# DMA transposes, LN2 statistics on GpSimd and own buffers for the last chunks in a pre-LN attention and gated-MLP block

## The chip, the cores and the metric

The kernel runs on one core of a Trainium2 chip. The metric is device microseconds of one execution. Before the change the kernel took 938.5 us (median of three runs, 938.18 to 938.94).

## The reference, cut to what matters

```python
def _A_ref(x, wqkv, wo):              # 2048 rows, 640 columns, 32 heads of 20
    q, k, v = split(x @ wqkv)
    p = softmax(q k^T * 20 ** -0.5)
    return (p v) @ wo
def _B_ref(x, w_gate, w_up, w_down):  # 640 -> 1728 -> 640
    return (gelu(x @ w_gate) * (x @ w_up)) @ w_down
h  = x + _A_ref(layernorm(x), ...)
h2 = h + _B_ref(layernorm(h), ...)    # this layernorm is "LN2" below
```

(Names shortened; the cuts are of reshapes and dtypes.) All inputs are bf16. There are 2048 x 2048 x 32 exponentials, and that decides how the kernel is built.

## The kernel before

The kernel plans itself. A small list scheduler in Python takes every operation with a modelled duration, the engine it runs on, what it reads and writes, and a priority; it simulates the five engines and writes the resulting order into the program. The program gives each engine its own queue in that fixed order, with waits on semaphores. So an edit of one part can change the order of everything that comes after it.

The query rows are split into chunks of 512, 512, 256, 256, 256, 128 and 128 rows (chunks 0 to 6). Attention of chunk c on ScalarE (the exponentials) runs beside the background work of earlier chunks: output projection, residual addition, LN2 and the MLP. VectorE computes a part of the exponentials as well, with integer arithmetic, in pairs of tiles of seven instructions. Priorities are numbers, lower first:

```python
P_QK, P_PV, P_PRO, P_EPI, P_BG = 0, 1, 1.5, 2, 3

def transposes(src, rkeys, dst, wkey, banks, prio, evac, after=()):
    bk = Bank(*banks)                       # one of the two PSUM banks for background work
    for a in range(NA):                     # five 128 x 128 transposes on TensorE
        op("pe", lambda eng, a=a: eng.transpose(bank16(bk, D)[:, 128*a:128*a+128],
                                                src[:, a*128:(a+1)*128], ident[:]), ...)
    if evac == "act": ...                   # the last chunk ("tail"): ScalarE evacuates
    else:
        op("dve", lambda eng: eng.tensor_copy(dst, v()), c_dve(D, 0.54), prio, ...)

def base(c):                                # which of four row-tile buffers a chunk starts at
    return 2 * (c % 2) if CHUNKS[c][1] < 512 else 0

def post(c, banks, tail):
    p = P_EPI if tail else P_BG
    for tt in range(tb, tb + nt):           # per 128 rows
        transposes(o_nat[:, tt, :], ..., oT[...], ..., P_EPI, ev)     # attention output
        for hf in range(2):                 # output projection, then residual addition
            list(chain(bk, key, 320, [(oT[...], wo[...]) for a in range(NA)], ..., p))
            op("dve", ... h_sb = psum + h_sb ..., p)
        ln_stats(h_sb[:, tt, :], t, ..., p)                            # bn_stats, bn_aggr
    ln_rsqrt(q0 // 128, nt, p, table=tail)  # 14 tiny VectorE operations: 1/sqrt by Newton steps
    for tt in range(tb, tb + nt):
        ln_apply("dve", h_sb[:, tt, :], xn_t[:, t % 2, :], ...)
        transposes(xn_t[:, t % 2, :], ..., hnT[...], ..., p, ev)       # LN2 output
    # gate matmuls -> VectorE copies -> GELU in batches on ScalarE -> up matmuls, product on
    # VectorE -> down matmuls -> residual addition on VectorE -> store      (all at P_BG)
```

Equal priorities are served in the order of creation.

Of the kernel before, what the change touches and what calls it, by code (L numbers as in the profile page):

```python
# [317 lines left out]
def bass_sequential_preLN__mha_block__glu_gated_geglu__prompt_kernel(  # L318
# [12 lines left out]
    with ExitStack() as es:  # L331
# [186 lines left out]
        def ln_rsqrt(t0, n, prio, table=False, sqrt=False):  # L518

            y = rs[:, t0:t0 + n]  # L520
            a, b = nw[:, 0, 0:n], nw[:, 1, 0:n]
            ts = range(t0, t0 + n)
            k16, ks = ("mv16", t0), ("sd16", t0)
            rk = [("rs", t) for t in ts]
            d = lambda fn, r, w: op("dve", fn, 0.17, prio, reads=r, writes=w)
            d(I("tensor_copy", mv16[:, t0:t0 + n, :], mv[:, t0:t0 + n, :]), [("mv", t) for t in ts], [k16])
            d(I("tensor_scalar", sd16[:, t0:t0 + n], mv16[:, t0:t0 + n, 1], LN_EPS, None, ALU.add), [k16], [ks])
            d(I("tensor_copy", mu[:, t0:t0 + n], mv16[:, t0:t0 + n, 0]), [k16], [("mu", t) for t in ts])
            if sqrt:
                op("act", I("activation", sd16[:, t0:t0 + n], sd16[:, t0:t0 + n], ACT.Sqrt), 0.2, 1, reads=[ks], writes=[ks])  # L530
                d(I("reciprocal", y, sd16[:, t0:t0 + n]), [ks], rk)
                return
            if table:
                op("act", I("activation", sd16[:, t0:t0 + n], sd16[:, t0:t0 + n], ACT.Sqrt), 0.2, -1, mode="sqrt", reads=[ks],
                   writes=[ks])
                d(I("reciprocal", y, sd16[:, t0:t0 + n]), [ks], rk)
                return
            d(I("tensor_copy", a, sd16[:, t0:t0 + n]), [ks], ["nw0"])
            d(I("tensor_scalar", b.bitcast(I32), a.bitcast(I32), 1, None, ALU.logical_shift_right), ["nw0"], ["nw1"])
            d(I("tensor_scalar", y.bitcast(I32), b.bitcast(I32), -1.0, RSQRT_MAGIC, ALU.mult, ALU.add), ["nw1"], rk)  # L540
            for _ in range(2):
                d(I("tensor_tensor", b, y, y, ALU.mult), rk, ["nw1"])
                d(I("scalar_tensor_tensor", out=b, in0=b, scalar=-0.5, in1=a, op0=ALU.mult, op1=ALU.mult),
                  ["nw0", "nw1"], ["nw1"])
                d(I("scalar_tensor_tensor", out=y, in0=b, scalar=1.5, in1=y, op0=ALU.add, op1=ALU.mult),
                  ["nw1"] + rk, rk)
            d(I("tensor_tensor", sd16[:, t0:t0 + n], a, y, ALU.mult), ["nw0"] + rk, [ks])
            d(I("reciprocal", y, sd16[:, t0:t0 + n]), [ks], rk)

        def ln_apply(eng, src, dst, dkey, t, rkeys, prio):  # L550
            if eng == "act":
# [6 lines left out]
        def transposes(src, rkeys, dst, wkey, banks, prio, evac, after=()):  # L558
            bk = Bank(*banks)
            key = ("bk", id(bk), sc_id())  # L560
            for a in range(NA):
                op("pe", lambda eng, a=a: eng.transpose(  # L562
                    bank16(bk, D)[:, 128 * a:128 * a + 128], src[:, a * 128:(a + 1) * 128], ident[:]),
                   0.055, prio, mode="full", reads=list(rkeys) + ["ident"], writes=[key], acq=[bk] if a == 0 else [],
                   after=tuple(sc.rd.get(wkey, ())) if a == 0 else ())
            v = lambda: bank16(bk, D).rearrange("p (a e) -> p a e", a=NA)
            if evac == "act":
                op("act", lambda eng: eng.activation(dst, v(), ACT.Copy), c_act(D), prio, reads=[key],
                   writes=[wkey], rel=[bk], after=after)
            else:  # L570
                op("dve", lambda eng: eng.tensor_copy(dst, v()), c_dve(D, 0.54), prio, reads=[key], writes=[wkey],
                   rel=[bk], after=after)

        _id = [0]

# [191 lines left out]
        while i < len(tiles):  # L767
# [4 lines left out]
            nd = D_PER_SLOT[c] if s_ else D_SLOT0  # L772
            units.append(tiles[i:i + len(bs)])
            ubank.append(bs[0])
            i += len(bs)
            want = min(nd, (k[0] - D_FIRST) * nd // D_SPAN + 1) if k[0] >= D_FIRST else 0
            if k[1] < want and tiles[i][0] == s_:
                dtile.append(tiles[i])
# [158 lines left out]


        def base(c):
            return 2 * (c % 2) if CHUNKS[c][1] < 512 else 0  # L940

        def epilogue(s_, bk):
            s = s_ % 2
# [29 lines left out]
        def prefetch(c):  # L973
# [1 line left out]
            nt = nq // 128  # L975
            tb = base(c)
            op("sp", I("dma_start", h_sb[:, tb:tb + nt, :], x_hbm[q0:q0 + nq, :].rearrange("(t p) d -> p t d", p=128)), 0.08, P_EPI,
               writes=[("h", tb + tt, hf) for tt in range(nt) for hf in range(2)], sem="xr", lat=2.0 + nq * 0.0034,
               after=tuple(e_ops) + tuple(w_readers) if c == 0 else ())

        def post(c, banks, tail):
# [1 line left out]
            q0, nq = CHUNKS[c]  # L983
            nt = nq // 128
            tb = base(c)
            kb = 7 * (tb // 2)
            first = tuple(e_ops) + tuple(last_qk[0]) + tuple(d_ops) if c == 0 else ()
            ev = "act" if tail else "dve"
            for tt in range(tb, tb + nt):
                t = q0 // 128 + tt - tb  # L990
                i = t % 2
                transposes(o_nat[:, tt, :], [("on", g, tt) for g in range(NG)], oT[:, :, tt * 128:(tt + 1) * 128],
                           ("hnT", tt), banks, P_EPI, ev, after=first)
                for hf in range(2):
                    bk = Bank(*banks)
                    key = ("bk", sc_id())
# [13 lines left out]
            for tt in range(tb, tb + nt):  # L1010
                t = q0 // 128 + tt - tb
                ln_apply("dve", h_sb[:, tt, :], xn_t[:, t % 2, :], ("xn", t % 2), t, [("h", tt, 0), ("h", tt, 1)], p)
                transposes(xn_t[:, t % 2, :], [("xn", t % 2)], hnT[:, :, tt * 128:(tt + 1) * 128], ("hnT", tt),
                           banks, p, ev, after=first)
            p = P_BG
            hk = [("hnT", tt) for tt in range(tb, tb + nt)]
            hdone = []
# [16 lines left out]
            def cols(k):  # L1034
                return min(512, (NF - k * fn_) * nq)

            if tail:
                for k in range(nb):
                    i = k % 2
                    bg, kg = mms(k, wg, "wg", hdone[k - 2:k - 1] if k >= 2 else ())  # L1040
                    w = cols(k)
                    s16, fv = zb[:, i, 0:w], ha_f[:, 512 * (kb + k):512 * (kb + k) + w]
                    op("act", lambda eng, bg=bg, s16=s16, w=w: eng.activation(s16, bank(bg, w), ACT.Gelu_apprx_tanh),
                       c_act(w), -1, mode="gelu", reads=[kg], writes=[("zb", i)], rel=[bg])
                    bu, ku = mms(k, wu, "wu", ())
                    hdone.append(op("dve", lambda eng, bu=bu, s16=s16, fv=fv, w=w: eng.tensor_tensor(
                        fv, s16, bank(bu, w), ALU.mult), c_dve(w), p, reads=[ku, ("zb", i)], writes=[("ha", kb + k)],
                        rel=[bu]))
            else:

                cp, gl = [], []
                for k in range(nb):
                    bg, kg = mms(k, wg, "wg", tuple(sc.rd.get(("ha", kb + k), ())))
                    w = cols(k)
                    fv = ha_f[:, 512 * (kb + k):512 * (kb + k) + w]
                    cp.append(op("dve", lambda eng, bg=bg, fv=fv, w=w: eng.tensor_copy(fv, bank(bg, w)), c_dve(w), p,
                                 reads=[kg], writes=[("ha", kb + k)], rel=[bg], after=first))
                for ks in [list(range(i, min(i + 4, nb))) for i in range(0, nb, 4)]:
                    w = 512 * (ks[-1] - ks[0]) + cols(ks[-1])
                    fv = ha_f[:, 512 * (kb + ks[0]):512 * (kb + ks[0]) + w]  # L1060
                    gl.append(op("act", I("activation", fv, fv, ACT.Gelu_apprx_tanh), c_act(w) + 0.04, -1, mode="gelu",
                                 reads=[("ha", kb + k) for k in ks], writes=[("ha", kb + k) for k in ks], after=cp))
                for k in range(nb):
                    w = cols(k)
                    fv = ha_f[:, 512 * (kb + k):512 * (kb + k) + w]
                    bu, ku = mms(k, wu, "wu", (sc.lw[("ha", kb + k)],))
                    hdone.append(op("dve", lambda eng, bu=bu, fv=fv, w=w: eng.tensor_tensor(fv, fv, bank(bu, w),  # L1067
                                                                                                 ALU.mult),
                                    c_dve(w), p, reads=[ku, ("ha", kb + k)], writes=[("ha", kb + k)], rel=[bu]))
            for tt in range(tb, tb + nt):  # L1070
                t = q0 // 128 + tt - tb
                i = t % 2
                for hf in range(2):
                    bk = Bank(*banks)
                    key = ("bk", sc_id())
                    for f in range(NF):
                        o = 512 * kb + f * nq + (tt - tb) * 128
                        op("pe", lambda eng, f=f, o=o, hf=hf, bk=bk: eng.matmul(  # L1078
                            bank(bk, 320), ha_f[:, o:o + 128], wd[:, f, hf * 320:(hf + 1) * 320],
                            start=(f == 0), stop=(f == NF - 1)), c_mm(320), p, mode="full", util=0.133, reads=[("ha", kb + f // fn_), "wd", "wdz"],  # L1080
                           writes=[key], acq=[bk] if f == 0 else [], after=hdone[-2:] if f == 0 else ())
                    op("dve", lambda eng, bk=bk, tt=tt, hf=hf, i=i: eng.tensor_tensor(
                        ob[:, i, hf * 320:(hf + 1) * 320], bank(bk, 320), h_sb[:, tt, hf * 320:(hf + 1) * 320], ALU.add),
# [86 lines left out]
```

## Time and profile before

The page of the kernel before, its busy times and its chain of waits by engine:

```profile
PE 860.0 (92%) x10297; PEld 365.5 (39%) x10297; DVE 829.1 (88%) x1807; ACT 883.7 (94%) x799; POOL 12.8 (1%) x33
...
ACT 77%; PE 15%; DVE 8%; issue 1%; DVEq 0%
```

PE is TensorE's matmuls, PEld its weight loads, DVE VectorE, ACT ScalarE, POOL GpSimd. Three engines look full at once, so the share of the whole span decides nothing. It has to be split by stage. Windows of the kernel before, each with its length, the busy time of each engine, the granted clock and the DMA share:

```profile
core 0: us, PE busy (x) PEld busy (x) DVE busy (x) ACT busy (x) POOL busy (x), PEclk, DMA share, GB/s
...
475.00:690.00 215.00, 200.05 (x2663) 82.13 (x2661) 197.30 (x420) 214.94 (x189) 0.00 (x0) 1.00 0.03 8
...
797.00:850.00 53.00, 49.77 (x1151) 31.52 (x1149) 48.69 (x116) 52.94 (x46) 0.00 (x0) 1.00 0.03 9
...
887.00:912.00 25.00, 21.49 (x231) 15.91 (x219) 16.25 (x48) 10.83 (x10) 0.00 (x0) 1.00 0.06 19
912.00:939.00 27.00, 23.87 (x341) 21.31 (x341) 10.29 (x23) 6.16 (x9) 0.00 (x0) 1.00 0.05 16
```

In the middle ScalarE is busy for all but 0.06 us of 215. After 887 us it idles and TensorE works. That last stretch is the tail, and what fills it is seen in ScalarE's timeline, where the GELU batches (written `rege<-rege`) tell how late the MLP of each chunk is:

```profile
350.76 6.46 ACT L339 ACTIVATE rege<-rege 128x2048 bf16<-128x2048 bf16 x4
...
579.24 6.46 ACT L339 ACTIVATE rege<-rege 128x2048 bf16<-128x2048 bf16 x4
...
727.74 3.28 ACT L339 ACTIVATE rege<-rege 128x2048 bf16<-128x2048 bf16 x2 [1.37 <-DVE rege L1056]
...
807.31 3.28 ACT L339 ACTIVATE rege<-rege 128x2048 bf16<-128x2048 bf16 x2
...
888.74 3.28 ACT L339 ACTIVATE rege<-rege 128x2048 bf16<-128x2048 bf16 x2
...
894.26 1.45 ACT L339 ACTIVATE rege<-ps 128x1536 bf16<-128x1536 f32 x1
```

These are chunks 0 to 4 (start in us, duration, and in brackets the idle time before it and who ended it); the last line is the last exponential, which ends at 895.7. The last chunk's residual rows are fetched late. The queue of DMA issues before:

```profile
839.65 0.34 SPq L339 DMA_DIRECT2D rege<-in_A_x_dram  x1
...
907.06 0.34 SPq L339 DMA_DIRECT2D rege<-in_A_x_dram  x1
```

The load at 907 us is that of chunk 6, which shares its buffer with chunk 4 and so waits for chunk 4's last read.

### The profile page before, as it was taken

To read this page: it belongs to the slowest core of one execution; us is meant where nothing else is said; L and a number is where in the kernel's file an instruction comes from. 1 tells how busy PE (TensorE), PEld (TensorE's weight loads), DVE (VectorE), ACT (ScalarE), POOL (GpSimd) and SP (SyncE) were. 2 spreads that over 40 slices of the span, in tenths; PEclk is the share of its full clock that TensorE was granted. 3 is DMA by queue.
4 is the path that set the end of the run, shared out by engine and by line. 5 is a ranking of instruction groups with operands and counts; after the bars stand their busy time and mean duration, and the time that the engine had idled before them with its cause. 6 is when DMAs were issued, how large, how long until landed. Compare 5 with 4: busy or idle time off the path is not lost.

```text
span 939.2 us, 23514 instructions
## 1 busy us (share of the span) xinstructions
PE 860.0 (92%) x10297; PEld 365.5 (39%) x10297; DVE 829.1 (88%) x1807; ACT 883.7 (94%) x799; POOL 12.8 (1%) x33
## 2 busy tenths in 40 slices
PE   3998999999998999998898998999999899999998
PEld 2432322222222222332243333344434446566577
DVE  7859999999899998987799999798999989989953
ACT  6899999999999999999999999999999999999931
POOL 5000000000000000000000000000000000000000
PEclk9999999999999999999999999999999999999999
DMA  7311010322630000001000000000000000000000
GB/s 253 91 24 40 19 52 18 89 65 65 198 124 1 1 2 1 1 22 37 1 2 1 2 1 1 1 3 29 30 2 1 2 20 13 3 17 10 3 22 16
DMA packets 22046, 30.12 MB, mean 32 GB/s; under 512 B 1964, under 2 KB 19464, under 8 KB 21944
## 3 DMA queue, kind: packets, MB, share of 16 engines
q1 hardware_dynamic: 21944, 28.63, 9.9%
q8 instruction: 80, 1.31, 0.6%
q14 instruction: 22, 0.18, 0.1%
HBM read 20.12 MB, written 8.09 MB: 30 GB/s over the span
## 4 chain that ended last, share of the span: by engine, by line
ACT 77%; PE 15%; DVE 8%; issue 1%; DVEq 0%
ACT pts L339 50%; ACT rege L339 26%; PE ps L1027 4%; PE ps L614 3%; PE ps L850 2%; PE ps L1078 2%; PE ps L339 2%; DVE rege L339 2%; DVE qt_all L339 2%; ACT L339 1%; DVE rege L810 1%; DVE stats L339 1%; PE ps L562 1%; DVE qt_all L810 0%; DVE kt_all L339 0%
## 5 line engine op out<-in xcount | busy, mean ns | idle before, releaser
L339 ACT ACTIVATE pts<-ps 128x1536 bf16<-128x1536 f32 x480 | 574.0, 1383 | 6.1 <-PE ps L850 4.3
L850 PE MATMUL ps<-qt_all,kt_all 32*128 32x256 bf16 (+2 forms) x3584 | 303.3, 289 | 42.7 <-ACT pts L339 28.1
L339 ACT ACTIVATE rege<-ps 128x1536 bf16<-128x1536 f32 x239 | 300.6, 1383 | 4.5 <-PE ps L339 3.1
L850 PEld LDWEIGHTS ps<-qt_all,kt_all 32*128 32x128 bf16 x3584 | 95.7, 92 | 276.4 <-ACT pts L339 163.9
L339 DVE TENSOR_TENSOR qt_all<-qt_all 128x1024 bf16<-128x1024 bf16 (+1 forms) x240 | 164.3, 685 | 3.2
L1027 PE MATMUL ps<-rege,regw 128*128 128x256 bf16 (+2 forms) x980 | 152.9, 289 | 9.5 <-ACT rege L339 4.3
L339 PE MATMUL ps<-pts,v_all 128*21 128x256 bf16 (+2 forms) x2098 | 139.2, 291 | 0.5 <-DVE rege L339 0.5
L810 DVE TENSOR_SCALAR rege<-ps 128x512 int16<-128x512 f32 x154 | 105.5, 685 | 27.5 <-PE ps L850 26.5
L339 DVE TENSOR_SCALAR qt_all<-qt_all 128x1024 bf16<-128x1024 int16 (+1 forms) x288 | 116.0, 419 | 2.0
L339 PE MATMUL ps<-rege,v_all 128*21 128x256 bf16 (+2 forms) x1294 | 113.3, 292 | 0.0
L1027 PEld LDWEIGHTS ps<-rege,regw 128*128 128x128 bf16 x980 | 72.8, 97 | 63.5 <-issue 20.8
L614 PE MATMUL ps<-regw 128*128 128x512 bf16 (+1 forms) x360 | 87.6, 354 | 2.0 <-DVE v_all L747 0.7
L1078 PE MATMUL ps<-regw,rege 128*128 128x320 bf16 x448 | 78.0, 301 | 1.9 <-DVE rege L1067 0.8
L810 DVE TENSOR_SCALAR qt_all<-ps 128x512 int16<-128x512 f32 x96 | 65.7, 687 | 4.0 <-PE ps L850 2.9
L339 DVE TENSOR_SCALAR rege<-rege 128x1024 int16<-128x1024 int16 (+2 forms) x166 | 67.3, 422 | 1.1
L339 DVE TENSOR_TENSOR rege<-rege 128x1024 bf16<-128x1024 bf16 (+3 forms) x103 | 65.7, 645 | 0.9
L339 PE MATMUL ps<-kt_all,zer 128*32 128x512 bf16 x740 | 65.7, 389 | 0.0
L339 PEld LDWEIGHTS ps<-pts,v_all 128*21 128x21 bf16 x2098 | 50.2, 91 | 37.5 <-issue 31.0
L1078 PEld LDWEIGHTS ps<-regw,rege 128*128 128x128 bf16 x448 | 36.9, 98 | 32.6 <-issue 15.2
L339 PEld LDWEIGHTS ps<-rege,v_all 128*21 128x21 bf16 x1294 | 41.1, 91 | 19.7 <-issue 13.8
L614 PEld LDWEIGHTS ps<-regw 128*128 128x128 bf16 x360 | 28.7, 99 | 45.8 <-issue 21.9
L1067 DVE TENSOR_TENSOR rege<-rege,ps 128x512 bf16<-128x512 bf16 (+1 forms) x53 | 35.9, 679 | 10.5 <-PE ps L1027 9.6
(92 smaller groups left out, 596.7 us busy)
## 6 DMA issues: line engine op xcount, KB each, us to landing
rege<-in_A_x_dram SPq DMA_DIRECT2D x6, 640.0 KB, 5.1
q_rows<-regw SPq DMA_DIRECT2D x20, 128.0 KB, 1.7
out_dram<-rege SPq DMA_DIRECT2D x16, 160.0 KB, 2.1
regw<-in_B_w_gate_dram SPq DMA_DIRECT2D x1, 2160.0 KB, 12.6
regw<-in_B_w_up_dram SPq DMA_DIRECT2D x1, 2160.0 KB, 17.6
regw<-in_B_w_down_dram SPq DMA_DIRECT2D x1, 2080.0 KB, 23.0
kt_all<-k_rows SPq DMA_DIRECT2D x12, 160.0 KB
qt_all<-q_rows SPq DMA_DIRECT2D x12, 160.0 KB
```

The lines of the kernel that those rows point to most:

```text
L339: return lambda eng: getattr(eng, method)(*args, **kwargs)
L562: op("pe", lambda eng, a=a: eng.transpose(bank16(bk, D)[:, 128 * a:128 * a + 128], src[:, a * 128:(a + 1) * 128], ident[:]), 0.055, prio, ...
L614: yield op("pe", lambda eng, l=l, r=r, k=k: eng.matmul(bank(bk, n), l, r, start=(k == 0), stop=(k == len(steps) - 1)), c_mm(n), prio, mode ...
L810: d_ops.append(op("dve", lambda eng: eng.tensor_scalar(v[:, 512 * h:512 * h + 512], bank(b), EXP_MUL, -32000.0, ALU.mult, ALU.max), c_dve( ...
L850: return lambda eng: eng.matmul(out()[:, kk * nq:(kk + 1) * nq], kt_all[32 * j:32 * j + 32, g, kt * 128:(kt + 1) * 128], qt_all[32 * j:32 ...
L1027: op("pe", lambda eng, a=a, f=f, fi=fi: eng.matmul(bank(bk)[:, fi * nq:(fi + 1) * nq], w[:, a, F0[f]:F0[f] + 128], hnT[:, a, 128 * tb:128 ...
L1067: hdone.append(op("dve", lambda eng, bu=bu, fv=fv, w=w: eng.tensor_tensor(fv, fv, bank(bu, w), ALU.mult), c_dve(w), p, reads=[ku, ("ha", k ...
L1078: op("pe", lambda eng, f=f, o=o, hf=hf, bk=bk: eng.matmul(bank(bk, 320), ha_f[:, o:o + 128], wd[:, f, hf * 320:(hf + 1) * 320], start=(f = ...
```

## The change

The intent is to take work from VectorE: transposes of the attention output (chunks 1 to 5) and of the LN2 output (chunks 0 to 5) go to the DMA engines, 26 of the 32; the LN2 statistics chain of these chunks goes to GpSimd; and chunks 5 and 6 get buffers of their own so that the last chunk need not wait for chunk 4. Cut to its core:

```diff
 def ln_rsqrt(...):
+            v = lambda fn, r, w: op("dve", fn, 0.17, prio, reads=r, writes=w)
+            d = v if table or sqrt else lambda fn, r, w: op(POOL, fn, 0.25, prio, reads=r, writes=w)
-            (shift, multiply-add; two scalar_tensor_tensor per Newton step)
+            (multiply-add; tensor_tensor, tensor_scalar, tensor_tensor per Newton step)
-            d(I("reciprocal", y, sd16[:, t0:t0 + n]), [ks], rk)
+            v(I("reciprocal", y, sd16[:, t0:t0 + n]), [ks], rk)
+        def dma_transposes(src, rkeys, dst, wkey, after=()):
+            op("sp", I("dma_start_transpose", dst, src), 1.25, P_EPI, reads=rkeys, writes=[wkey], sem=f"xp{wkey[1]}", lat=2.0, after=after)
 def base(c):
+            n = CHUNKS[c][1]
+            if n == 128:
+                return 2 + (c == len(CHUNKS) - 1)
-            return 2 * (c % 2) if CHUNKS[c][1] < 512 else 0
+            return 2 * (c % 2) if n < 512 else 0
 def post(c, banks, tail):
+                if tail or c == 0: transposes(o_nat[:, tt, :], ...)
+                else:              dma_transposes(o_nat[:, tt, :], ...)
...
+                if tail: transposes(xn_t[:, t % 2, :], ...)
+                else:    dma_transposes(xn_t[:, t % 2, :], ...)
```

Cut from this diff: the residual load gets one semaphore per chunk, and the keys of the MLP's hidden buffer become finer, both for the own buffers.

More of the change, by code (lines that the diff above doesn't have):

```diff
@@ L524, in ln_rsqrt @@
             rk = [("rs", t) for t in ts]
-            d = lambda fn, r, w: op("dve", fn, 0.17, prio, reads=r, writes=w)
+            v = lambda fn, r, w: op("dve", fn, 0.17, prio, reads=r, writes=w)
+            d = v if table or sqrt else lambda fn, r, w: op(POOL, fn, 0.25, prio, reads=r, writes=w)
             d(I("tensor_copy", mv16[:, t0:t0 + n, :], mv[:, t0:t0 + n, :]), [("mv", t) for t in ts], [k16])
@@ L535, in ln_rsqrt @@
                    writes=[ks])
-                d(I("reciprocal", y, sd16[:, t0:t0 + n]), [ks], rk)
+                v(I("reciprocal", y, sd16[:, t0:t0 + n]), [ks], rk)
                 return
             d(I("tensor_copy", a, sd16[:, t0:t0 + n]), [ks], ["nw0"])
-            d(I("tensor_scalar", b.bitcast(I32), a.bitcast(I32), 1, None, ALU.logical_shift_right), ["nw0"], ["nw1"])
-            d(I("tensor_scalar", y.bitcast(I32), b.bitcast(I32), -1.0, RSQRT_MAGIC, ALU.mult, ALU.add), ["nw1"], rk)
+            d(I("tensor_scalar", y.bitcast(I32), a.bitcast(I32), -0.5, RSQRT_MAGIC, ALU.mult, ALU.add), ["nw0"], rk)
             for _ in range(2):
                 d(I("tensor_tensor", b, y, y, ALU.mult), rk, ["nw1"])
-                d(I("scalar_tensor_tensor", out=b, in0=b, scalar=-0.5, in1=a, op0=ALU.mult, op1=ALU.mult),
-                  ["nw0", "nw1"], ["nw1"])
-                d(I("scalar_tensor_tensor", out=y, in0=b, scalar=1.5, in1=y, op0=ALU.add, op1=ALU.mult),
-                  ["nw1"] + rk, rk)
+                d(I("tensor_tensor", b, b, a, ALU.mult), ["nw0", "nw1"], ["nw1"])
+                d(I("tensor_scalar", b, b, -0.5, 1.5, ALU.mult, ALU.add), ["nw1"], ["nw1"])
+                d(I("tensor_tensor", y, y, b, ALU.mult), ["nw1"] + rk, rk)
             d(I("tensor_tensor", sd16[:, t0:t0 + n], a, y, ALU.mult), ["nw0"] + rk, [ks])
-            d(I("reciprocal", y, sd16[:, t0:t0 + n]), [ks], rk)
+            v(I("reciprocal", y, sd16[:, t0:t0 + n]), [ks], rk)
         def ln_apply(eng, src, dst, dkey, t, rkeys, prio):
@@ L774, in bass_sequential_preLN__mha_block__glu_gated_geglu__prompt_kernel @@
             ubank.append(bs[0])
-            i += len(bs)
+            i += len(units[-1])
             want = min(nd, (k[0] - D_FIRST) * nd // D_SPAN + 1) if k[0] >= D_FIRST else 0
@@ L977, in prefetch @@
             op("sp", I("dma_start", h_sb[:, tb:tb + nt, :], x_hbm[q0:q0 + nq, :].rearrange("(t p) d -> p t d", p=128)), 0.08, P_EPI,
-               writes=[("h", tb + tt, hf) for tt in range(nt) for hf in range(2)], sem="xr", lat=2.0 + nq * 0.0034,
+               writes=[("h", tb + tt, hf) for tt in range(nt) for hf in range(2)], sem=f"xr{c}", lat=2.0 + nq * 0.0034,
                after=tuple(e_ops) + tuple(w_readers) if c == 0 else ())
@@ L985, in post @@
             tb = base(c)
-            kb = 7 * (tb // 2)
+            hb = 1792 * tb
             first = tuple(e_ops) + tuple(last_qk[0]) + tuple(d_ops) if c == 0 else ()
-            ev = "act" if tail else "dve"
             for tt in range(tb, tb + nt):
@@ L991, in post @@
                 i = t % 2
-                transposes(o_nat[:, tt, :], [("on", g, tt) for g in range(NG)], oT[:, :, tt * 128:(tt + 1) * 128],
-                           ("hnT", tt), banks, P_EPI, ev, after=first)
+                if tail or c == 0:
+                    transposes(o_nat[:, tt, :], [("on", g, tt) for g in range(NG)], oT[:, :, tt * 128:(tt + 1) * 128],
+                               ("hnT", tt), banks, P_EPI, "act" if tail else "dve", after=first)
+                else:
+                    dma_transposes(o_nat[:, tt, :], [("on", g, tt) for g in range(NG)], oT[:, :, tt * 128:(tt + 1) * 128],
+                                   ("hnT", tt), after=first)
                 for hf in range(2):
@@ L1012, in post @@
                 ln_apply("dve", h_sb[:, tt, :], xn_t[:, t % 2, :], ("xn", t % 2), t, [("h", tt, 0), ("h", tt, 1)], p)
-                transposes(xn_t[:, t % 2, :], [("xn", t % 2)], hnT[:, :, tt * 128:(tt + 1) * 128], ("hnT", tt),
-                           banks, p, ev, after=first)
+                if tail:
+                    transposes(xn_t[:, t % 2, :], [("xn", t % 2)], hnT[:, :, tt * 128:(tt + 1) * 128], ("hnT", tt),
+                               banks, p, "act", after=first)
+                else:
+                    dma_transposes(xn_t[:, t % 2, :], [("xn", t % 2)], hnT[:, :, tt * 128:(tt + 1) * 128], ("hnT", tt),
+                                   after=first)
             p = P_BG
@@ L1035, in cols, with hv, hkeys @@
                 return min(512, (NF - k * fn_) * nq)
+            def hv(k, w):
+                return ha_f[:, hb + 512 * k:hb + 512 * k + w]
+            def hkeys(k):
+                return [("ha", u) for u in range((hb + 512 * k) // 256, (hb + 512 * k + cols(k)) // 256)]
             if tail:
@@ L1041, in post @@
                     w = cols(k)
-                    s16, fv = zb[:, i, 0:w], ha_f[:, 512 * (kb + k):512 * (kb + k) + w]
+                    s16, fv = zb[:, i, 0:w], hv(k, w)
                     op("act", lambda eng, bg=bg, s16=s16, w=w: eng.activation(s16, bank(bg, w), ACT.Gelu_apprx_tanh),
@@ L1046, in post @@
                     hdone.append(op("dve", lambda eng, bu=bu, s16=s16, fv=fv, w=w: eng.tensor_tensor(
-                        fv, s16, bank(bu, w), ALU.mult), c_dve(w), p, reads=[ku, ("zb", i)], writes=[("ha", kb + k)],
+                        fv, s16, bank(bu, w), ALU.mult), c_dve(w), p, reads=[ku, ("zb", i)], writes=hkeys(k),
                         rel=[bu]))
@@ L1052, in post @@
                 for k in range(nb):
-                    bg, kg = mms(k, wg, "wg", tuple(sc.rd.get(("ha", kb + k), ())))
+                    bg, kg = mms(k, wg, "wg", tuple(x for key in hkeys(k) for x in sc.rd.get(key, ())))
                     w = cols(k)
-                    fv = ha_f[:, 512 * (kb + k):512 * (kb + k) + w]
+                    fv = hv(k, w)
                     cp.append(op("dve", lambda eng, bg=bg, fv=fv, w=w: eng.tensor_copy(fv, bank(bg, w)), c_dve(w), p,
-                                 reads=[kg], writes=[("ha", kb + k)], rel=[bg], after=first))
+                                 reads=[kg], writes=hkeys(k), rel=[bg], after=first))
                 for ks in [list(range(i, min(i + 4, nb))) for i in range(0, nb, 4)]:
                     w = 512 * (ks[-1] - ks[0]) + cols(ks[-1])
-                    fv = ha_f[:, 512 * (kb + ks[0]):512 * (kb + ks[0]) + w]
+                    fv = hv(ks[0], w)
                     gl.append(op("act", I("activation", fv, fv, ACT.Gelu_apprx_tanh), c_act(w) + 0.04, -1, mode="gelu",
-                                 reads=[("ha", kb + k) for k in ks], writes=[("ha", kb + k) for k in ks], after=cp))
+                                 reads=sum(map(hkeys, ks), []), writes=sum(map(hkeys, ks), []), after=cp))
                 for k in range(nb):
                     w = cols(k)
-                    fv = ha_f[:, 512 * (kb + k):512 * (kb + k) + w]
-                    bu, ku = mms(k, wu, "wu", (sc.lw[("ha", kb + k)],))
+                    fv = hv(k, w)
+                    bu, ku = mms(k, wu, "wu", (sc.lw[hkeys(k)[-1]],))
                     hdone.append(op("dve", lambda eng, bu=bu, fv=fv, w=w: eng.tensor_tensor(fv, fv, bank(bu, w),
                                                                                                  ALU.mult),
-                                    c_dve(w), p, reads=[ku, ("ha", kb + k)], writes=[("ha", kb + k)], rel=[bu]))
+                                    c_dve(w), p, reads=[ku] + hkeys(k), writes=hkeys(k), rel=[bu]))
             for tt in range(tb, tb + nt):
@@ L1076, in post @@
                     for f in range(NF):
-                        o = 512 * kb + f * nq + (tt - tb) * 128
+                        o = hb + f * nq + (tt - tb) * 128
                         op("pe", lambda eng, f=f, o=o, hf=hf, bk=bk: eng.matmul(
                             bank(bk, 320), ha_f[:, o:o + 128], wd[:, f, hf * 320:(hf + 1) * 320],
-                            start=(f == 0), stop=(f == NF - 1)), c_mm(320), p, mode="full", util=0.133, reads=[("ha", kb + f // fn_), "wd", "wdz"],
+                            start=(f == 0), stop=(f == NF - 1)), c_mm(320), p, mode="full", util=0.133, reads=hkeys(f // fn_) + ["wd", "wdz"],
                            writes=[key], acq=[bk] if f == 0 else [], after=hdone[-2:] if f == 0 else ())
```

## The prediction

> **What bounds it now.** To 36 us: the prologue, left alone. From 36 to 887 us ScalarE is the bound: the windows show it busy 214.9 of 215 us (475 to 690) and 52.9 of 53 (797 to 850); it has 77% of the chain of waits. It keeps its 719 exponentials at 1.13 us each, so nothing freed on VectorE or TensorE shortens this stage. From 887 to 939 comes the tail, with ScalarE mostly idle (busy 10.8 of 25 us, then 6.2 of 27) and TensorE busy.
>
> The tail is long because the MLP of earlier chunks is in arrears. ScalarE's timeline has GELU batches at 350, 579, 728, 807 and 889 us; attention for chunk 4 ended near 796, so its GELU is 90 us late, and the up and down products of chunk 4 and nearly all of chunk 5's MLP run after 887. VectorE sets that pace: 91 to 97% busy in the middle windows, with its own exponentials ahead of the MLP in priority. TensorE's 92% includes 740 padding matmuls, so it has room. Chunk 4's statistics chain, 14 operations of 0.16 us, lasts from 811.3 to 831.8, queued on VectorE.
>
> **What the change does.**
> - 26 of the 32 transposes go to DMA. VectorE loses 26 evacuations of 0.482 us, 12.5 us; TensorE 130 matmuls. Each becomes a 160 KB transfer; plain ones of 128 to 160 KB take 1.7 to 2.1 us to landing. I estimate 3 us with issue; the Trainium skill, "DMA: Bandwidth & Descriptors", "Latency and other measured facts", names about 2 us fixed, which agrees.
> - Six statistics chains, 13 operations of 0.16 us each, leave VectorE: 12 us.
> - So 25 us of VectorE are freed, against arrears of near 17 us at 887 (11 products of 0.685 us, evacuations of 0.685 and 0.49). The arrears should mostly vanish.
> - Own buffers: the last chunk's residual load is issued only at 907.1, after chunk 4's last read; its addition waits from 904.6 to 909.35. Those 4.7 us go.
>
> **Against it.** The skill's "SBUF — State Buffer" ("Who interferes with whom") says GpSimd and two-port or two-input VectorE instructions exclude each other. I expect chains of 5 to 10 us on GpSimd; VectorE's reciprocal waits for them in order, and TensorE waits in order for transposes that land later than the static order assumes. I allow 3 to 6 us for such stalls. If chunk 5's GELU moves before the last exponentials, it adds 1.7 us and two table loads of 1.28.
>
> **Sum.** The last exponential ends at 895.7; then 896 to 902. From there the last chunk needs: output, projection, LN2 14 us, 140 gate and up matmuls 7.8, GELU and product 1.3, down 4.0, store 2.7: 30 us, against 43.5 now. That is 926 to 932. Median 928.5 us, 1.1% faster; range 919.5 to 941. Chances: over 2% faster 0.08, within 2% 0.86, over 2% slower 0.06.
>
> **What would show it.** VectorE's busy time falls by 20 to 25 us; exponentials keep 1.13 us and end within 896 to 902; the GELUs of chunks 2 to 4 come tens of microseconds earlier; chunk 4 is finished before 887; the tail after the last exponential is 28 to 35 us; the last residual load comes before 900.
>
> **What would make it wrong.** DMA transposes of 5 us or more, or GpSimd chains beyond 10 us, holding up the in-order TensorE and VectorE queues so that ScalarE gets gaps: 940 or worse. Arrears that persist because the order, not VectorE, set them: 935 to 938. Chunk 5 still interleaved with the last chunk in the tail.

## More of the kernel before

Every run quoted here was fast, with a mean granted TensorE clock of 0.994 to 1.0.

Even the third digit of the clock matters. The traces show stretches of 3.4 us in which half the clock was granted. The profiled run of the kernel before has one, and so took 940.96 us, while that of the kernel after (929.34) has none. The window of the kernel before that holds it:

```profile
273.80:277.20 3.40, 3.40 (x27) 0.95 (x27) 2.84 (x7) 2.37 (x3) 0.00 (x0) 0.50 0.01 2
```

(Start and end in us, length, busy time of the engines, then the clock, 0.50.) The 29 runs of the kernel before that were timed beside the experiments took 938.1 to 939.6 us at clock 1.0 and 940.9 to 941.2 at 0.998. A difference of 1 to 3 us between two profiles has to be read with that in mind.

## The result, and the profile after

The kernel after took 929.81 us (median of four runs, 928.71 to 931.52), beside 938.72 for the kernel before (four runs). The ratio is 0.9902, with a 95% interval of 0.988 to 0.9925. Ratios here are the mean time of one kernel's fast runs over that of the other's fast runs of the same rounds, so they are not quite the ratio of the quoted medians. The range held it, and it lies 1.3 us from the forecast. The parts of the forecast fared less well, as the profile after shows. Its busy times and its chain by engine:

```profile
PE 837.1 (90%) x10069; PEld 356.9 (38%) x10126; DVE 811.3 (87%) x1703; ACT 883.2 (95%) x799; POOL 39.1 (4%) x117
...
ACT 73%; PE 14%; DVE 9%; DMA 2%; POOL 1%; issue 1%; SPq 0%
```

VectorE lost 17.8 us, less than the 20 to 25 announced. The same windows after:

```profile
475.00:690.00 215.00, 194.74 (x2597) 82.59 (x2613) 194.55 (x399) 214.05 (x188) 9.34 (x28) 1.00 0.07 16
...
797.00:850.00 53.00, 49.04 (x1226) 29.57 (x1228) 47.79 (x107) 53.00 (x48) 3.66 (x14) 1.00 0.11 25
...
887.00:912.00 25.00, 24.09 (x369) 19.97 (x367) 13.65 (x33) 9.87 (x12) 0.00 (x0) 1.00 0.07 21
912.00:939.00 27.00, 12.04 (x144) 9.82 (x142) 3.77 (x7) 1.58 (x3) 0.00 (x0) 0.96 0.04 13
```

The middle is as full as it was; TensorE's work after 912 us has halved. (The kernel ends at 927.4, so the clock of 0.96 in the last line is that of the time behind its end.) ScalarE's timeline after, the same batches:

```profile
349.13 6.46 ACT L339 ACTIVATE rege<-rege 128x2048 bf16<-128x2048 bf16 x4
...
561.22 6.46 ACT L339 ACTIVATE rege<-rege 128x2048 bf16<-128x2048 bf16 x4
...
696.62 3.28 ACT L339 ACTIVATE rege<-rege 128x2048 bf16<-128x2048 bf16 x2
...
770.86 3.28 ACT L339 ACTIVATE rege<-rege 128x2048 bf16<-128x2048 bf16 x2
...
869.69 3.28 ACT L339 ACTIVATE rege<-rege 128x2048 bf16<-128x2048 bf16 x2
...
888.62 1.59 ACT L339 ACTIVATE rege<-ps 128x1536 bf16<-128x1536 f32 x1
```

Chunks 2 and 3 gained 31 and 36 us, chunk 4 only 19. The last exponential ends at 890.2, 5.5 us earlier than before, and the tail behind it lasts 37.2 us against 43.5 (span less that end). Summing ScalarE's idle stretches of over 0.05 us between its first and last exponential gives 8.2 us before and 3.8 after. Of the 8.2, 1.4 lie in or right behind the half-clock stretch of that profile and are not the change's doing, so some 3 of the 5.5 us are. Another 0.7 is the start of the first exponential, 36.4 before and 35.7 after; over all profiled runs it starts between 35.0 and 36.4, so that much is not the change. DMA issues after:

```profile
790.88 3.10 SPq L339 DMA_TRANSPOSE rege<-o_nat  x2
802.25 0.34 SPq L339 DMA_DIRECT2D rege<-in_A_x_dram  x1
...
811.33 0.34 SPq L339 DMA_DIRECT2D rege<-in_A_x_dram  x1
```

The last residual load now comes at 811.3 and not at 907. The transposes, from the profile's list of DMA issues (count, median us from issue to landing):

```profile
rege<-xn_t SPq DMA_TRANSPOSE x15, 2.6
...
rege<-o_nat SPq DMA_TRANSPOSE x11, 2.7
```

With issue and flight in 2.6 to 2.7 us in the median they are a little faster than the 3 us estimated, and within the 1.25 + 2.0 us for which the planner leaves room; three of the 26 took longer, up to 4.3. Little waited for them. VectorE's waits after, the two that are new:

```profile
DVE rs L339 <- POOL sd L339: 5.0, 5, 2.3
...
DVE xn_t L339 <- DMA rege<-xn_t: 2.1, 1, 2.1
```

(us in total, times, longest.) The chains on GpSimd took 4.4 to 6.5 us from first start to last end; on VectorE the same six had taken 4.2 to 20.3 us, because they stood in a full queue.

### The profile page after: what moved, and what is told of

It is laid out like the page before. It is cut to its first block, busy times and chain, and to the rows that moved or that the text cites. A ratio compares the mean times of both kernels' runs of the same rounds, so it can differ in the third digit from the quotient of the medians.

```text
span 927.4 us, 23141 instructions
## 1 busy us (share of the span) xinstructions
PE 837.1 (90%) x10069; PEld 356.9 (38%) x10126; DVE 811.3 (87%) x1703; ACT 883.2 (95%) x799; POOL 39.1 (4%) x117
## 2 busy tenths in 40 slices
DMA packets 39517, 34.36 MB, mean 37 GB/s; under 512 B 19436, under 2 KB 36936, under 8 KB 39416
## 4 chain that ended last, share of the span: by engine, by line
ACT 73%; PE 14%; DVE 9%; DMA 2%; POOL 1%; issue 1%; SPq 0%
ACT pts L339 46%; ACT rege L339 25%; PE ps L1039 3%; PE ps L616 3%; DVE qt_all L339 3%; PE ps L1096 3%; PE ps L852 3%; PE ps L339 2%; DVE rege L339 2%; DMA regw<-in_A_wqkv_dram 1%; ACT L339 1%; DVE rege L812 1%; DVE qt_all L812 1%; POOL nw L339 0%; PE ps L561 0%
## 5 line engine op out<-in xcount | busy, mean ns | idle before, releaser
L1039 PE MATMUL ps<-rege,regw 128*128 128x256 bf16 (+2 forms) x957 | 149.2, 287 | 10.3 <-ACT rege L339 2.8
L616 PE MATMUL ps<-regw 128*128 128x512 bf16 (+1 forms) x342 | 82.1, 349 | 3.8 <-issue 1.3
L339 PEld LDWEIGHTS ps<-pts,v_all 128*21 128x21 bf16 x2098 | 50.2, 91 | 37.9 <-issue 31.7
L339 PE MATMUL ps<-kt_all,zer 128*32 128x512 bf16 x680 | 56.4, 384 | 0.0
## 6 DMA issues: line engine op xcount, KB each, us to landing
regw<-in_B_w_gate_dram SPq DMA_DIRECT2D x1, 2160.0 KB, 13.3
```

The lines of the kernel that those rows point to most:

```text
L339: return lambda eng: getattr(eng, method)(*args, **kwargs)
L616: yield op("pe", lambda eng, l=l, r=r, k=k: eng.matmul(bank(bk, n), l, r, start=(k == 0), stop=(k == len(steps) - 1)), c_mm(n), prio, mode ...
L1039: op("pe", lambda eng, a=a, f=f, fi=fi: eng.matmul(bank(bk)[:, fi * nq:(fi + 1) * nq], w[:, a, F0[f]:F0[f] + 128], hnT[:, a, 128 * tb:128 ...
```

## The experiments

The open questions were: which of the three parts earns the 9 us; whether it is VectorE's time (theory V) or what else a TensorE transpose occupies (theory T); and why chunk 4 was still late (VectorE again, or the order of the queue, theory O). Every kernel was re-planned by its own scheduler. They were timed in three sessions of five rounds, each on another chip and each with the kernel before beside them (e1 to e4, e5 to e8, e9 to e12); no run of the kernel after is there, so it is compared with them by the ratios. "Chunk 4 done" is the end of its last down matmul in the trace; all times are in us.

| run | median | ratio to before | 95% interval | VectorE busy | last exponential ends | tail | chunk 4 done |
|---|---|---|---|---|---|---|---|
| before | 938.7 | | | 829.1 | 895.7 | 43.5 | 910 |
| after | 929.8 | 0.9902 | 0.9880–0.9925 | 811.3 | 890.2 | 37.2 | 899 |
| e1_dma | 931.0 | 0.9911 | 0.9897–0.9925 | 818.4 | 891.5 | 37.9 | 902 |
| e2_pool | 937.6 | 0.9992 | 0.9975–1.0008 | 820.4 | 884.7 | 51.1 | 906 |
| e3_buf | 937.3 | 0.9983 | 0.9969–0.9997 | 828.7 | 893.2 | 41.9 | 908 |
| e4_nobuf | 929.8 | 0.9898 | 0.9884–0.9912 | 811.6 | 890.9 | 37.2 | 900 |
| e5_nodma | 934.9 | 0.9959 | 0.9947–0.9971 | 820.5 | 884.2 | 48.9 | 907 |
| e6_nopool | 929.8 | 0.9905 | 0.9892–0.9918 | 818.2 | 889.7 | 37.9 | 901 |
| e7_addv | 942.1 | 1.0021 | 1.0007–1.0036 | 820.0 | 900.8 | 39.4 | 906 |
| e8_addp | 931.5 | 0.9929 | 0.9917–0.9940 | 812.4 | 891.9 | 37.5 | 905 |
| e9_relief_after | 926.8 | 0.9873 | 0.9858–0.9887 | 705.1 | 885.3 | 38.8 | 878 |
| e10_relief_before | 925.5 | 0.9862 | 0.9848–0.9877 | 720.5 | 886.3 | 37.1 | 895 |
| e11_order | 927.6 | 0.9885 | 0.9869–0.9902 | 811.5 | 893.8 | 31.9 | 893 |
| e12_best | 921.9 | 0.9826 | 0.9812–0.9841 | 809.3 | 890.3 | 29.8 | 880 |

In e2 and e5 the exponentials end early and the tail is long by the same amount, because there the planner put a GELU batch behind the last exponential and not before it. So the end of the exponentials is read together with the tail, never alone.

### e1 to e6: one part alone, and all but one part

Edits: e1 keeps only the DMA transposes, e2 only the GpSimd chain, e3 only the own buffers; e4, e5 and e6 are the full change with one part taken back. In short:

```diff
 e4, e1, e2 (buffers as before):
-            if n == 128:
-                return 2 + (c == len(CHUNKS) - 1)
 e5, e2, e3 (TensorE transposes as before):
-                if tail or c == 0:
+                if True:
                     transposes(o_nat[:, tt, :], ...)        (and so for xn_t)
 e6, e1, e3 (chain on VectorE as before):
   the whole of ln_rsqrt as it was in the kernel before
```

e1_dma:

> Only the DMA transposes; statistics and buffers as before. Theory V (the gain comes from VectorE time freed, and the evacuations and the statistics are half each of it): about half of the gain of 9 us, a ratio to before of 0.994 to 0.996. Rival T (it comes from what the transposes held beside VectorE: a background PSUM bank, TensorE turns, the wait from one to the next): nearly all of it, 0.989 to 0.992. A change of order alone may move any of these by some 2 us.

e2_pool:

> Only the statistics chain on GpSimd; transposes and buffers as before. Theory V: about half of the gain, 0.994 to 0.996. Rival T: 0.998 to 1.000, VectorE busy some 8 us less and the end unmoved.

e3_buf:

> Only the own buffers for the last two chunks. As predicted (the 4.7 us wait of the last chunk's residual addition goes): 0.995. Rival (that wait lay beside TensorE work that had to be done in the tail anyway): 0.999 to 1.000, the load issued before 860 us and the tail as long as before.

e4_nobuf:

> The whole change without the own buffers. If they are worth their 4.7 us in the full change: 0.995 to before. If not: 0.990, like the full change, with the residual load of the last chunk again after chunk 4's last read, near 900 us.

e5_nodma:

> The whole change without the DMA transposes (statistics on GpSimd and own buffers stay). Theory V: about half of the gain, 0.994 to 0.996 to before. Rival T: 0.998 to 1.000.

e6_nopool:

> The whole change with the statistics chain back on VectorE in the old form. Theory V: 0.994 to 0.996. Rival T: 0.989 to 0.992, like the full change.

Measured: the transposes alone give 0.9911, nearly all of the full change's 0.9902 (the one run of e1 at clock 1.0 took 929.6 us, as the kernel after does). The chain alone is not told apart from nothing (0.9992), and without it (e6) the change is as fast as with it. The buffers alone are worth 0.2%, and taking them out of the full change (e4) changes nothing, although the load comes late again (893.2 us). So the 4.7 us wait that the prediction wanted to collect was real but not worth its length: TensorE had other matmuls to do in the meantime (in the kernel before it is busy for all of 904.46 to 910.32 us, mostly with down matmuls).

By the letter this favours T over V, for V had given the chain half of the gain. But V's shares came from adding recorded durations: 12.5 us for evacuations and 12 for the chain. VectorE's busy time fell by 10.7 us in e1 and by 8.7 in e2. The evacuations stay worth more, yet not by enough to explain 7.7 us against 1.1. Chain and buffers together (e5) give 0.4%, and 0.1 and 0.2 each alone; with intervals of 0.1 to 0.2% on each, that is no clear departure from a sum. Part of such differences is re-planning, whose size e11 and e12 show.

### e7 and e8: give back one half of a transpose's cost

Edits, at the place of each DMA transpose in the full change:

```diff
 e7 (VectorE's load, nothing waits for it; the scratch tile takes words that nothing used):
+            op("dve", I("tensor_tensor", spare[:], src, src, ALU.max), c_dve(D, 0.54), prio, reads=rkeys, writes=["spare"])
 e8 (TensorE's load and the bank, nobody reads the result):
+            bk = Bank(*banks)
+            for a in range(NA):
+                op("pe", lambda eng, a=a: eng.transpose(bank16(bk, D)[:, 128*a:128*a+128], src[:, a*128:(a+1)*128], ident[:]),
+                   0.055, prio, mode="full", ..., acq=[bk] if a == 0 else [], rel=[bk] if a == NA - 1 else [])
```

> The full change, and for each of the 26 DMA transposes a VectorE instruction of the same 640 columns (two bf16 inputs in SBUF, some 0.48 us) that nothing waits for: VectorE's load of the transposes is back, TensorE's and the PSUM bank's is not. Theory V: 4 to 5 us of the gain go, 0.994 to 0.996. Rival T: no more than 1 or 2 us go, 0.990 to 0.992.

> The full change, and for each of the 26 DMA transposes the five TensorE transposes of before into a background PSUM bank, which nobody reads: TensorE's load and the bank's are back, VectorE's is not. Theory V: unmoved within 1 or 2 us, 0.989 to 0.992. Rival T: 4 us or more of the gain go, 0.994 to 0.998.

Measured: with the 26 VectorE instructions (0.485 us each in the trace) the median is 942.1 us, 12.3 above the kernel after. The clock has a part in that: four of the six runs had a mean of 0.995, and the only one at 1.0 took 937.9 us, some 8.5 above the runs of the kernel after at 1.0 (929.3). So the instructions take about the whole gain; that they make the kernel slower than before is not shown, nor whether the edit itself brings about the half-clock stretches. The TensorE transposes with their bank cost 1.7 us; the ratio, 0.9929, lies between the two ranges and nearer to V's. Some 8 us against 2 speaks for V as to what counts in a transpose. e8 does not give back all that T named: its bank comes free when the transposes end, and nothing waits for their result, while in the kernel before bank and result waited for VectorE's copy. But the form of the loss was not what V had in mind. Chunk 3's down matmuls end at 817 us in e7, near the kernel after's 811 and far from the 856 of before, so the arrears of that chunk did not come back. The loss is in ScalarE's stage: idle stretches of 13.3 us between first and last exponential where the kernel after has 3.8 (2.2 of the 13.3 are in or right behind half-clock stretches). Its waits in e7:

```profile
ACT pts L339 <- PE ps L339: 7.6, 5, 4.6
...
ACT rege L339 <- PE ps L339: 3.2, 4, 1.5
```

and the same two in the kernel after, of which only the second is long enough to be listed near the top:

```profile
ACT rege L339 <- PE ps L339: 1.5, 1, 1.5
```

The matmuls waited for are in the trace the products with V, behind which the next exponential starts. The longest such wait, 4.56 us, ends at 604.4 us. TensorE did not stand still in it (the window's columns are as above):

```profile
599.90:604.40 4.50, 4.50 (x55) 2.83 (x55) 4.35 (x11) 0.00 (x0) 0.00 (x0) 1.00 0.23 44
```

For 3.1 us of it TensorE ran 21 down matmuls that its queue has ahead of those products; some of these read VectorE's exponentials. That the planner filled in the down matmuls because VectorE was late is inferred from this place and from the edit; the profile names only TensorE. e7 is no exact restoration: its instruction reads two SBUF inputs and not PSUM, and 11 of the 26 stand ahead of the MLP in priority. It shows that 12 us of VectorE instructions can cost 8 us or more, not that they always do.

### e9 and e10: give VectorE time

Both give a wrong result (relative error 0.04): two of the seven instructions of each exponential pair on VectorE are left out, in the kernel after (e9) and in the kernel before (e10).

```diff
-            d(I("tensor_scalar", df, fi, -E1 / OCT, -E0, ALU.mult, ALU.add), 0.265, ["df"], ["df"])
-            d(I("tensor_tensor", dw, dw, df, ALU.mult), 0.53, ["df", "dw"], ["dw"])
```

> Wrong result on purpose. The full change, with two of the seven instructions of every exponential pair on VectorE left out (0.42 and 0.685 us, 125 pairs: some 125 us of VectorE less), ScalarE and TensorE keep theirs. Theory V (VectorE's time still sets the arrears): the MLP of chunk 4 ends before the last exponential and the kernel takes 918 to 924 us. Rival O (after the change the order of the background work sets them: chunk 4's projection waits for chunk 3's down products): 927 to 930, chunk 4 still done near 899.

> Wrong result on purpose. The kernel before with the same two instructions left out. If VectorE's time is all that the change's transposes freed to effect, before and after now agree within 2 us (the change is worth nothing once VectorE has time). If the transposes also gave TensorE turns, a bank or shorter waits that matter, before stays 5 us or more behind after with the same omission.

Measured: with VectorE relieved, before and after take 925.5 and 926.8 us. The change is then worth nothing (before is 1.3 us ahead, but three of e9's four runs had a clock of 0.996 and all of e10's 0.998; the one of e9 at 0.998 took 925.5, as e10 does). So 13 us of the kernel before go when VectorE has time, and the change's gain lies within them. Together with e7 and e8 this is the best evidence for V, though each of the four kernels has its own plan. By itself it doesn't exclude that the transposes held something that matters only while VectorE is late.

e9 also tells what is left. Its 106 us of further VectorE time brought only 3.0 us, between what V and O had foretold. The idle stretches of ScalarE vanished (0.2 us), chunk 4 was done at 878 us, before the last exponential, as V said; but the tail was no shorter, 38.8 us. Two half-clock stretches (from 889.5 and from 899.8) lie in it and show in the clock of its window:

```profile
887.00:912.00 25.00, 20.79 (x248) 17.79 (x249) 10.45 (x28) 5.17 (x7) 0.00 (x0) 0.86 0.06 14
```

Half of twice 3.4 us, 3.4, is the most that they can have cost (an estimate), so at full clock the tail would be 35 us or more, at most 2 shorter than the kernel after's. The reason is in TensorE's timeline of e9, around the end of chunk 4's down matmuls (`regw,rege`):

```profile
877.67 0.31 PE L1094 MATMUL ps<-regw,rege 128*128 128x320 bf16 x1
877.82 0.84 PE L616 MATMUL ps<-wo,rege 128*128 128x320 bf16 x5
```

The second half of chunk 5's output projection (`wo,rege`) runs directly behind chunk 4's last down matmul, 25 us after the first half began at 853. It had the same priority as the MLP and a later creation, so it queued; everything of chunk 5 behind it, LN2 and the whole MLP, fell into the tail. That is O. The kernel after shows the same for chunk 4: its transposed attention output was issued at 790.9 (shown above), and its projection began at 814, just after chunk 3's down matmuls ended. TensorE's timeline of the kernel after:

```profile
810.06 0.72 PE L1096 MATMUL ps<-regw,rege 128*128 128x320 bf16 x4
...
814.36 0.58 PE L616 MATMUL ps<-wo,rege 128*128 128x320 bf16 x3
```

### e11 and e12: change the order

e11 lets projection, residual addition and LN2 go ahead of the MLP of the chunk before. The projection must then also wait for the residual's load, or it could hold both background banks while the addition waits for a load that waits for older work; a first form without that wait could not be planned at all (the planner ends with "no operation can start") and was never run. e12 adds three planning constants, found by trying several hundred settings in the kernel's own planner. No instruction of the computation is added or removed in either; only the planner's padding matmuls, which multiply with zeros (680 in the kernel after, 640 in e11, 688 in e12), and the loads of ScalarE's function tables (12, 14 and 13 behind the first exponential) change with the plan.

```diff
 e11 and e12:
+EPI_FROM = 2
-            p = P_EPI if tail else P_BG
+            p = P_EPI if tail or c >= EPI_FROM else P_BG
-                                              for a in range(NA)], [("hnT", tt), "wo"], p))
+                                              for a in range(NA)], [("hnT", tt), "wo"], p, after=(sc.lw[("h", tt, hf)],)))
 e12 alone:
-D_FIRST, D_SPAN = 1, 16
+D_FIRST, D_SPAN = 0, 16
-        def c_dve(n, rate=1.0625):
+        def c_dve(n, rate=1.05):
-            op("sp", I("dma_start_transpose", dst, src), 1.25, P_EPI, ..., lat=2.0, after=after)
+            op("sp", I("dma_start_transpose", dst, src), 1.25, P_EPI, ..., lat=2.3, after=after)
```

> The full change, and from chunk 2 on the output projection, residual addition and LN2 go ahead of the MLP of the chunk before (priority of the epilogue; the projection then also waits for its residual to be loaded). Theory O: chunk 4's statistics come near 800 us and not 824 to 831, its down products end some 10 us earlier, 925 to 928 us. Theory V alone: the same work in another order, 929 to 932.

> The order of e11, and three constants of the kernel's own planning changed (VectorE rate 1.05 for 1.0625, transposes 0.3 us later, first VectorE exponential one unit earlier in a slot), no instruction added or removed. Theory O: 920 to 925 us, because planned VectorE gaps are filled tighter and chunk 4 is done before the last exponential. If such constants only shuffle: 926 to 930.

Measured: e11 927.6 us, e12 921.9 (correct both). e11 lies in O's range, 2.2 us below the kernel after, though the intervals of the two ratios overlap; chunk 4's statistics come at 806 to 810 us and its down products end 6.6 us earlier, a little less than O had said. In e12 chunk 4's projection starts at 792.6 us, in the midst of chunk 3's down matmuls. TensorE's timeline of e12:

```profile
791.52 0.45 PE L1097 MATMUL ps<-regw,rege 128*128 128x320 bf16 x2
792.60 0.30 PE L617 MATMUL ps<-wo,rege 128*128 128x320 bf16 x1 [0.27 <-issue]
...
800.78 0.43 PE L1097 MATMUL ps<-regw,rege 128*128 128x320 bf16 x2
```

and the last two windows of e12 together hold 26.7 us of TensorE work, against 36.1 in the kernel after and 45.4 before:

```profile
887.00:912.00 25.00, 21.92 (x366) 18.45 (x365) 12.33 (x31) 12.64 (x15) 0.00 (x0) 1.00 0.03 9
912.00:939.00 27.00, 4.79 (x43) 3.29 (x40) 1.83 (x4) 0.38 (x1) 0.00 (x0) 0.98 0.02 6
```

Its tail is 29.8 us. That equals the 30 us which the prediction had worked out for the last chunk alone, but is no check of them: chunk 5's GELU (891.6) and down matmuls (900.7 to 905.0) still lie in it. e11's tail is short as well, 31.9, but its exponentials end 3.6 us later than the kernel after's, mostly because its ScalarE idles 6.7 us and not 3.8 between them (one wait of 2.2 us ends at 648.7; its additional table loads lie in the tail). So O is confirmed as to the tail. e11 against e12 shows also how much planning alone moves: 5.7 us between two kernels that compute with the same instructions. Which of the three constants brought it was not separated, and no control with the constants but without the order was run. Differences of 1 to 3 us between other variants of this table are thus not put down to their parts.

## Why the prediction was right

**The total was right, by two errors that cancelled.** Said: last exponential at 896 to 902, then 30 us. Measured: 890.2, then 37.2. That the sum lies so close to the forecast is luck.

**"Nothing freed on VectorE or TensorE shortens this stage": wrong by some 3 us.** ScalarE was 99% busy, not 100%: 8.2 us of idle stretches before (1.4 of them from the half-clock stretch), 3.8 after, 0.2 in e9, 1.0 in e10. The window that the prediction cited was full; the sum over the stage was not.

**"I allow 3 to 6 us for such stalls": the term failed, no net stall came.** The chains on GpSimd took 4.4 to 6.5 us, at or below the low end of the 5 to 10 foreseen. VectorE did wait 5.0 us for them, but ScalarE's idle time fell all the same. The transposes landed in 2.6 to 2.7 us in the median, inside the planned time. Chunk 5's GELU did not move before the last exponentials.

**"25 us of VectorE are freed": 17.8 measured.** The prediction added recorded durations, and neighbouring VectorE instructions overlap in the record. Twenty-six evacuations of 0.482 us came to 10.7 us of busy time in e1 (0.41 each); the chain's 12 us came to 8.7 in e2. The Trainium skill says so, under "Perfetto Trace Analysis", section "Optimizing Scalar/DVE Operations": part of an instruction's recorded latency overlaps with the next instruction. The records of the kernel before add up to 939.4 us, while VectorE was busy for 829.1. The prediction should have used it.

**"The arrears should mostly vanish": half right; this is the step that failed.** VectorE did set them in the kernel before: e10 shows it. Chunk 3 was done at 811 us and no longer at 856 (this end alone is no measure of the gain: e1 and e6 keep it with 841 and 839). But chunk 4 was done at 899 us, 12 us after the 887 announced. VectorE's time still had a part in that: with VectorE relieved (e9) chunk 4 is done at 878, where O had said 899. The order had another: with the new priorities (e11) it is done at 893. And what kept the tail long was the order: a chunk's projection stood behind the older chunk's MLP (chunk 5's in e9), and e11's tail is 5 us shorter. The prediction named this under what would make it wrong, but counted work and not positions in the queue.

**"Those 4.7 us go": the wait went, the time did not.** The residual load moved from 907 to 811 us, and e4 is as fast as the full change.

**The three parts are far from equal.** The text gave evacuations and statistics about equal weight. The runs give the transposes 0.9 of the 1.0% and the statistics nothing that could be measured within the full change (e6). Why 8.7 us of freed VectorE time in e2 brought 1.1 us while 10.7 in e1 brought 7.7 is not settled. Re-planning is one candidate; another is that tiny instructions fill gaps that a long one can't.

## What to carry to other kernels

When one engine is full and the rest runs behind it in a fixed queue, ask of every saved microsecond whose queue it frees and what stands next in it; after the first bottleneck the order of the queue may be cheaper to change than more work is to remove (here 9 us by the change; another 2 by priorities alone, near the noise, and 8 with three planning constants changed as well). Test "engine X sets the pace" by taking work from X with a result that is wrong, in both kernels: if before and after meet, the change's gain lay within X's lack of time. Look at the clock of every profile before you read microseconds from it. And don't add up recorded durations of neighbouring instructions; take the busy time of a kernel without them.

## What the Trainium skill lacked or had wrong

- "VectorE: DVE Perf Modes", section "Rules for kernel authors", advises TensorE for a 128x128 transpose when a PSUM destination is fine, with 390 ns against 1309 ns for DMA in "The three transpose paths". By itself a DMA transpose was slower here, too (2.6 to 2.7 us for 128x640; five TensorE transposes 0.28 us and the copy 0.48). Yet moving 26 of them made the kernel 0.9% faster (e1), and e7 and e8 point to the PSUM evacuation of 0.482 us on a full VectorE as the cost that counted. The rule does not weigh that evacuation.
- "DMA: Bandwidth & Descriptors", section "DMA Transpose (X-bar)", has no latency for a small SBUF-to-SBUF transpose on trn2 (the 1309 ns above are for 128x128). Here 160 KB took 2.6 to 2.7 us from issue to landing, and the DMA packets rose from 22046 to 39517, 672 for each of the 26, nearly all of them under 512 B.
- "GPSIMD Engine Reference", section "Performance versus the Vector engine", gives elementwise times for 512 and 2048 elements only. The smallest operations (1 to 8 elements per partition) were recorded with 0.18 to 0.23 us undisturbed and up to 0.96 beside a busy VectorE; the same kind on VectorE with 0.14 to 0.17. A chain of 14, each waiting for the one before, took 4.4 to 6.5 us in the kernel after and 3.5 to 5.0 in e9, where VectorE had less to do. This fits the mutual exclusion in "SBUF — State Buffer", section "Who interferes with whom", which the prediction had cited. The trace of the kernel after shows it operation by operation: the 38 of the 84 that start while VectorE works on 128x1024 tiles in SBUF took 0.25 to 0.96 us, the other 46 took 0.18 to 0.23. No run measured the exclusion by itself.
